# Inputs with the heads of a position side by side in DRAM, and the input and gated tiles of a float32r feed-forward shifted by 192 bytes against its weights

## The chip, the cores and the metric

One Trainium2 chip, one of its cores. The metric is the device time of one execution in microseconds, as the median of the runs; what the host does with the arrays before the launch is outside it.

## The reference

A linear attention with a complex decay, followed by a gated feed-forward. There are 4 batches, 8 heads, 768 positions and 48 channels per head; the feed-forward has 3072 tokens, 384 inputs and 1536 hidden columns.

```python
mag = np.sqrt(a_re * a_re + a_im * a_im)
scale = np.minimum(mag, 0.999) / (mag + 1e-06)
a_re_n, a_im_n = (a_re * scale, a_im * scale)
...
for t in range(S):
    ar, ai = (a_re_n[:, :, t, :, None], a_im_n[:, :, t, :, None])
    new_re = ar * S_re - ai * S_im
    new_im = ar * S_im + ai * S_re
    kv = np.einsum('bhd,bhe->bhde', k[:, :, t], v[:, :, t])
    S_re, S_im = (new_re + kv, new_im)
    y[:, :, t] = np.einsum('bhd,bhde->bhe', q[:, :, t], S_re)
...
x = np.ascontiguousarray(attn_out.transpose(0, 2, 1, 3)).reshape(B * S, H * D)
...
g = x @ w_gate
silu = g * (1.0 / (1.0 + np.exp(-g)))
val = x @ w_val
return (silu * val @ w_out).astype(np.float32)
```

The inputs q, k, v, a_re and a_im come as (batch, head, position, channel) float32; the three weights come as float64 and reach the chip as pairs of 32-bit words.

## The kernel before, in words

**Work.** The sequence is cut into 24 slabs of 128 positions (6 chunks of 4 batches). Two slabs form one of 12 groups, g = 0 to 11. For a group, `stage_ops` loads a_re, a_im, q and k (positions on the partitions, heads and channels in the row, `load` at L342, issued by SP), takes logarithms and arctangents on ACT, sums them along the positions with matmuls against a triangle (L445), and scales q and k by the results. `slab_ops` turns q and k (six slabs with TensorE transposes, L569; later ones with DVE's 32x32 transposes and shuffling DMAs `T<-ww`, L598), loads v (`ldv`, L606), makes the scores (L618) and their product with v (L649, into p_py), and updates the carried state (L676). The copy of p_py to SBUF is the transposed input of the feed-forward: `xh`, its rounding to float32r (L658), and `xl`, the rest (L665), 3 k-tiles of 128 channels by 256 positions.

**Feed-forward.** `ffn_ops` runs a group's feed-forward in 12 blocks f of 128 hidden columns. For g > 0 a block has 18 matmuls at L829: gate and value, 3 k-tiles, and three products each (weights' high part with xh, high part with xl, low part with xh). The weight tile is the stationary operand (128 columns, 512 bytes of a partition), xh or xl the moving one (256 columns). ACT takes the silu (L835), DVE multiplies (L840), and `hh` and `hl` are again a float32r rounding and its rest (L299 or L301, L295). Then 6 matmuls at L863 add the block to the two output banks; here hh or hl is stationary (128 of its 256 columns) and the row of w_out moves (384 columns). Group 0 does the same with whole float32 numbers and a third of the matmuls.

**Weights.** `weight_ops` loads the 64-bit words of block f into a tile (L719) and joins them to float32 on DVE (c1 to c3, L728 to L736). `split_ops` later writes their high and low float32r parts (c4, c5) into the place of the block before: `place("w", f - 1)`. So block f reads the tile ww(f-1) and wo(f-1).

**Addresses.** `place` lets the weights of place f begin `STARTS[f]` floats (0 to 56, so 0 to 224 bytes) behind the start of their tile, and the tiles of xh, xl, hh and hl have no such offset. All these tiles come from one pool, one behind the other in each partition. From the start addresses that the program gives them, the weights of L829 lie behind xh and xl, modulo 512 bytes, by 0, 400, 416, 176, 320, 336, 352, 384, 416, 448, 96 and 392 bytes for the blocks f = 0 to 11. The stationary hh and hl of L863 lie behind the moving row of w_out by 0, 112, 224, 208, 192, 176, 160, 128, 352, 64, 416 and 120 bytes. All steps within a tile (k-tiles, high and low part, gate and value, the second half of hh) are multiples of 512 bytes, so the distance is the same for all matmuls of a block.

**Order.** `Planner.plan` puts all operations in one order from written-out costs and due times, which neither addresses nor the layout in DRAM enter; each engine takes its instructions in that order. SP issues every DMA: inputs, weights, and the small transfers through DRAM of a chunk's last row (`dr` and `dec`, L466 and L472; `fr`, L523; `cy`, L490). After group 1 the weights are also read once more for a check of their range (`range_ops`, L777 to L786), and a_re and a_im of the first chunk for another check (`sector_ops`, L800). `general` is a slow way for other data; it isn't taken here.

**Rows of DRAM.** In `x[b0:b0 + many, :, c * P:c * P + P, :]` a position's channels of one head are 48 floats, 192 bytes, and the next head's lie 768 positions further. A load of two slabs (384 KB) is 2048 pieces of 192 bytes.

Of the kernel before, what the change touches and what calls it, by code (L numbers as in the profile page):

```python
# [42 lines left out]

STARTS = {-1: 0, 0: 4, 1: 8, 2: 12, 3: 16, 4: 20, 5: 24, 6: 32, 7: 40, 8: 48, 9: 56, 10: 2, 11: 0}
HIGH, LOW, WHOLE = 0, 1, 2
# [131 lines left out]


def flat(t):
    return t.rearrange("p h d -> p (h d)")  # L180
# [10 lines left out]
def quick(ctx, tc, q, k, v, a_re, a_im, w_gate, w_val, w_out, out, count):  # L191
# [27 lines left out]
    def place(nm, f, dtype):  # L219

        at = STARTS[f]
        t = work.tile([P, 2 * WIDE[nm] + -(-at // 64) * 64], dtype, name=f"w{nm}{f}", tag=f"w{nm}{f}", bufs=1)
        return t[:, at:at + 2 * WIDE[nm]]

# [7 lines left out]
    def weight(nm, f, part):  # L232
# [5 lines left out]
        if nm == "o":  # L238
# [6 lines left out]
             "hh": ([P, 2 * P], F32R), "hl": ([P, 2 * P], F32R), "ost": ([P, DM], F32),  # L245
             "sc": ([P, 4, P], F32), "T": ([96, 2, H * P], F32), "dec": ([96, 4 * H], F32),
             "qs": ([P, 2 * H, 96], F32), "ks": ([P, 2 * H, 96], F32)}
# [27 lines left out]
    def new(tag, inst):  # L275
        if tag in fixed:
            t = fixed[tag][0]
        elif tag[0] in ("ww", "wo"):
            t = None
        elif tag in PSUMS:  # L280
            t = psum.tile([P, 512], F32, name="p_" + tag, tag=tag, bufs=2 if tag == "po" else slots[tag])
        else:
            shape, dt = SHAPE[tag]
            if isinstance(inst, tuple) and inst[0] in SPLIT:
                dt = F32R
            if tag == "xh" and inst == 0:
                dt = F32
            if tag == "xl" and isinstance(inst, str):
                dt = U32
            t = work.tile(shape, dt, name=tag, tag=tag, bufs=slots[tag])  # L290
        at_[tag, inst] = t
        return t
# [26 lines left out]
    def stage_ops(g, first, many):  # L319
# [19 lines left out]
        def load(t, x):  # L339
            def fn(e):  # L340
                b0 = 2 * bp + first
                nc.sync.dma_start(out=new(*tg(t)), in_=x[b0:b0 + many, :, c * P:c * P + P, :].rearrange("b h t d -> t (b h) d"))  # L342
            pl.add(f"ld_{t}{N}", {"SP": 0.55}, fn, deps=[held.get(t, "")], alloc=[tg(t)], lat=1.4, move=1.09 * many)
# [198 lines left out]
    def slab_ops(n):  # L542
# [61 lines left out]
        def ldv(e):  # L604
            at_["vt", n] = vts[n % 2]
            nc.sync.dma_start(out=vts[n % 2][:, :, 0:D], in_=v[b, :, c * P:c * P + P, :].rearrange("h t d -> t h d"))  # L606
        pl.add("ldv" + N, {"SP": 0.55}, ldv, deps=[f"ldv{n - 1}"] if n else [], alloc=[("vt", n)], lat=1.4, move=1.09)
# [182 lines left out]
    def sector_ops(g):  # L790
# [7 lines left out]
        for t, x, tags in (("re", a_re, both), ("im", a_im, parts)):  # L798
            def ld(e, x=x, t=t):
                nc.sync.dma_start(out=at(t).rearrange("p (h d) -> p h d", d=D), in_=x[b0:b0 + 2, :, 0:P, :].rearrange("b h t d -> t (b h) d"))  # L800
            pl.add(f"kl{t}" + N, {"SP": 0.55}, ld, alloc=tags, lat=1.4, move=2.18, deps=[f"c5{NF - 1}o", f"f2_0.{NF - 1}", f"c5{NF - 1}w", f"f1_0.{NF - 1}"])
# [149 lines left out]
def general(ctx, tc, q, k, v, a_re, a_im, w_gate, w_val, w_out, out):  # L951
# [7 lines left out]
    with ExitStack() as first:  # L959
# [13 lines left out]
        with tc.For_i(0, S, TB) as t0:  # L973
            part = {}
            for nm, src in (("q", q), ("k", k), ("re", a_re), ("im", a_im)):
                part[nm] = two.tile([P, TB, DQ], F32, name="g_" + nm)
                for j in range(4):
                    nc.sync.dma_start(out=part[nm][32 * j:32 * j + 32],
                                      in_=src.rearrange("b h t d -> (b h) t d")[:, bass.ds(t0, TB), j * DQ:(j + 1) * DQ])
            vv = two.tile([P, TB, D], F32, name="g_v")  # L980
            for j in range(4):
                nc.sync.dma_start(out=vv[32 * j:32 * j + 32], in_=v.rearrange("b h t d -> (b h) t d")[:, bass.ds(t0, TB), :])
            mag, den = two.tile([P, TB, DQ], F32, name="g_mag"), two.tile([P, TB, DQ], F32, name="g_den")
# [127 lines left out]
```

## Time and profile before

| | us |
|---|---|
| median of 3 runs | 662.51 (660.56 to 663.02) |
| span of the profiled execution, first to last instruction | 657.5 |
| the median less that span | 5.0 |
| TensorE matmuls (PE) busy | 622.8 (95% of the span) |
| weight loads (PEld) busy | 582.5 (89%) |
| VectorE (DVE) busy | 499.6 (76%) |
| ScalarE (ACT) busy | 398.2 (61%) |
| DMA queue of the loads and stores, share of 16 engines | 49.2% |

The profile gives the profiled execution's span, and no time of its own around it; the 5.0 us are the difference to the median of the runs shown. Busy time counts an instruction from its start to its modelled end, so matmuls that follow each other without a gap overlap in it. The trace names operands by tile, out<-in; at L829 `p_gv<-xh,ww` is a matmul with xh moving and ww stationary. [...]

### The profile page before, as it was taken

The numbers are of one execution on the slowest core, as the hardware profiler recorded it, in microseconds if no ns is written. First come the engines' busy times: TensorE is split into PE (matmuls) and PEld (weight loads), VectorE is DVE, ScalarE is ACT, GpSimd is POOL, SyncE is SP. The second block draws the span as 40 slices with busy tenths as digits, with TensorE's granted clock in tenths as the row PEclk, the third lists the DMA queues.
The fourth block names the chain that finished last, engine by engine and source line by source line (L and its number), as shares of the span: only waits on it lengthen the run. The fifth ranks groups of instructions, "written<-read, shape, count | busy, mean of one in ns | idle before, by whom it ended". The sixth has DMA issues, their size and how long they took to land.

```text
span 657.5 us, 15503 instructions
## 1 busy us (share of the span) xinstructions
PE 622.8 (95%) x6306; PEld 582.5 (89%) x6306; DVE 499.6 (76%) x923; ACT 398.2 (61%) x654; POOL 3.0 (0%) x9
## 2 busy tenths in 40 slices
PE   2689999999999999999999999999999999999996
PEld 0367787899998999999999999999999999999995
DVE  8799999989876976976976976966876966643332
ACT  7865159876885866756956756967847836211110
POOL 1000000000000000000000000000000000000000
PEclk9999999999999999999999999999999999999998
DMA  9999602356645655655655656645543530320000
GB/s 181 293 286 287 169 25 55 53 111 117 164 105 125 165 120 128 153 138 122 159 131 122 153 130 130 141 126 122 123 105 63 126 85 16 77 52 1 25 1 29
DMA packets 234932, 77.49 MB, mean 118 GB/s; under 512 B 208859, under 2 KB 230621, under 8 KB 234854
## 3 DMA queue, kind: packets, MB, share of 16 engines
q1 hardware_dynamic: 234854, 76.43, 49.2%
q8 instruction: 51, 0.84, 0.5%
q14 instruction: 27, 0.22, 0.1%
HBM read 57.47 MB, written 4.78 MB: 95 GB/s over the span
## 4 chain that ended last, share of the span: by engine, by line
PE 66%; DVE 16%; DMA 8%; ACT 5%; issue 3%; SPq 1%; DVEq 0%; ACTq 0%
PE p_gv L829 35%; PE p_po L863 17%; PE p_py L649 5%; PE p_ps L618 5%; ACT L946 2%; DMA wo<-in_moe_w_val_dram 2%; PE p_pm L676 2%; ACT s L350 2%; PE p_pm L445 2%; DVE xl L732 1%; DMA wo<-in_moe_w_out_dram 1%; DVE sg L840 1%; DVE s L295 1%; DVE sc L624 1%; SPq L719 1%
## 5 line engine op out<-in xcount | busy, mean ns | idle before, releaser
L829 PE MATMUL p_gv<-xh,ww 128*128 128x256 f32 x1596 | 314.7, 293 | 1.3 <-DVE sg L840 1.1
L829 PEld LDWEIGHTS p_gv<-xh,ww 128*128 128x128 f32 x1596 | 258.1, 189 | 9.8 <-DVE sg L840 3.2
L829 PE MATMUL p_gv<-xl,ww 128*128 128x256 f32 x726 | 203.6, 280 | 0.0
L946 ACT ACT_TABLE_LOAD x111 | 142.4, 1283 | 1.9
L829 PEld LDWEIGHTS p_gv<-xl,ww 128*128 128x128 f32 x726 | 136.6, 188 | 0.1
L835 ACT ACTIVATE sg<-p_gv 128x256 f32<-128x256 f32 x144 | 54.0, 382 | 136.3 <-PE p_gv L829 135.3
L863 PE MATMUL p_po<-wo,hh 128*128 128x384 f32 x484 | 127.0, 343 | 0.0
L840 DVE TENSOR_TENSOR sg<-sg,p_gv 128x256 f32<-128x256 f32 x144 | 58.7, 414 | 62.4 <-ACT sg L835 62.4
L863 PEld LDWEIGHTS p_po<-wo,hh 128*128 128x128 f32 x484 | 81.5, 188 | 2.3 <-issue 2.2
L863 PE MATMUL p_po<-wo,hl 128*128 128x384 f32 x242 | 81.6, 337 | 0.0
L295 DVE TENSOR_TENSOR hl<-sg,hh 128x256 fp32r<-128x256 f32 x132 | 54.4, 418 | 6.8 <-ACT hh L299 1.5
L618 PE MATMUL p_ps<-T 96*128 96x128 f32 x384 | 53.2, 279 | 0.0
L618 PEld LDWEIGHTS p_ps<-T 96*128 96x128 f32 x384 | 50.6, 196 | 0.9 <-ACT T L299 0.3
L863 PEld LDWEIGHTS p_po<-wo,hl 128*128 128x128 f32 x242 | 45.5, 188 | 0.0
L299 ACT CAST hh<-sg 128x256 fp32r<-128x256 f32 x49 | 19.7, 403 | 34.7 <-DVE sg L840 27.9
L350 ACT ACTIVATE s<-s 128x768 f32<-128x768 f32 x44 | 36.7, 842 | 5.2 <-DVE s L295 4.7
L781 DVE TENSOR_REDUCE flags<-wo 128x1 f32<-128x384 f32 x36 | 19.8, 549 | 25.2 <-DMA wo<-in_moe_w_val_dram 11.3
L649 PE MATMUL p_py<-sc,vt 128*32 128x128 f32 x768 | 37.1, 273 | 1.5 <-ACT xh L658 0.9
L624 DVE TENSOR_TENSOR sc<-p_ps,tri 128x512 f32<-128x512 f32 x48 | 32.7, 682 | 4.0 <-PE p_ps L618 3.6
L649 PE MATMUL p_py<-T,G 96*32 96x128 f32 x640 | 33.5, 281 | 0.0
L786 ACT ACTIVATE wo<-wo 128x384 f32<-128x384 f32 x36 | 20.2, 562 | 12.6 <-DMA wo<-in_moe_w_out_dram 5.7
L829 PE MATMUL p_gv<-xh,ww-1_412 128*128 128x256 f32 x132 | 26.1, 287 | 1.7 <-ACT xh L658 1.7
(134 smaller groups left out, 800.9 us busy)
## 6 DMA issues: line engine op xcount, KB each, us to landing
T<-ww SPq DMA_DIRECT2D x216, 64.0 KB, 2.1
wo<-in_moe_w_out_dram SPq DMA_DIRECT2D x24, 384.0 KB, 5.9
ww<-in_moe_w_gate_dram SPq DMA_DIRECT2D x12, 384.0 KB, 5.9
vt<-in_v_dram SPq DMA_DIRECT2D x24, 192.0 KB, 4.3
ww<-in_moe_w_val_dram SPq DMA_DIRECT2D x12, 384.0 KB, 6.7
out_dram<-ost SPq DMA_DIRECT2D x24, 192.0 KB, 2.3
wo<-in_moe_w_gate_dram SPq DMA_DIRECT2D x12, 384.0 KB, 3.6
wo<-in_moe_w_val_dram SPq DMA_DIRECT2D x12, 384.0 KB, 4.0
```

The costliest lines, as they stand in the source:

```text
L295: V[e].tensor_tensor(out=out, in0=a, in1=b, op=op)
L350: nc.scalar.activation(out=of(dst), in_=of(source), func=func, scale=scale, **kw)
L618: nc.tensor.matmul(out=ps[:, hh, :], lhsT=kT(4 * qd + hh), rhs=qT(4 * qd + hh), start=True, stop=True)
L624: nc.vector.tensor_tensor(out=s, in0=at_["ps", f"{n}.{qd}"].rearrange("p (h t) -> p h t", h=4), in1=mask.unsqueeze(1).to_broadcast([P, 4, ...
L649: nc.tensor.matmul(out=o, lhsT=l, rhs=r, start=opens, stop=closes, tile_position=(0, 32 * slot))
L781: nc.vector.tensor_reduce(out=flags[:, fl_lo + j:fl_lo + j + 1], in_=high(1), axis=AX.X, op=ALU.min, apply_absolute_value=True)
L786: nc.scalar.activation(out=high(0), in_=high(1), func=AF.Square, accum_out=flags[:, fl_hi + j:fl_hi + j + 1])
L829: nc.tensor.matmul(out=gv[:, i, :], lhsT=l, rhs=r, start=(m == 0), stop=(m == len(mm) - 1))
L835: nc.scalar.activation(out=new("sg", I), in_=at_["gv", I][:, 0:2 * P], func=AF.Silu)
L840: nc.vector.tensor_tensor(out=sg, in0=sg, in1=at_["gv", I][:, 2 * P:4 * P], op=ALU.mult)
L863: nc.tensor.matmul(out=po, lhsT=l[:, cs], rhs=weight("o", f, part), start=f == 0 and j == 0, stop=f == NF - 1 and j == len(products) - 1)
L946: nc.scalar.preload_act_table_set(op.load)
```

## The change

Three things. First, the host hands over the five attention inputs as (batch, position, head, channel). All heads of a position are then one run of 384 floats (1536 bytes), and the loads take it as one piece; the tile's rows are the same as before. Only v's tile keeps a pitch of 64 floats per head, so its destination still has pieces of 48 floats. Second, the weight tiles begin at the start of their places (no `STARTS`), and the tiles of xh, xl, hh and hl get 128 floats more, of which the data begin 48 floats (192 bytes) in. Third, the small `dec` tile is padded to 512 bytes. The order of the plan stays: none of its inputs is touched.

By the sizes in the code, every tile of that pool is then a multiple of 512 bytes (ww 6144, wo 3072, xh and xl 3584, hh and hl 1536, dec 512, and the rest 1024, 1536, 2048, 3072, 6144 or 8192). So the weights of L829 lie 320 bytes (512 - 192) behind xh and xl in all 12 blocks, and hh and hl lie 192 bytes behind w_out in all. Between two blocks, where the next stationary operand is hh under a moving xh, or ww under a moving w_out, the distance is 0. The tiles sc, T, ks and qs move by 128 bytes, modulo 512, against vt and G, which stay.

```diff
-STARTS = {-1: 0, 0: 4, 1: 8, 2: 12, 3: 16, 4: 20, 5: 24, 6: 32, 7: 40, 8: 48, 9: 56, 10: 2, 11: 0}
+SHIFT = 48
...
+def rows(x, b0, many, c):
+    return x[b0:b0 + many, c * P:c * P + P].rearrange("b t h d -> t b (h d)")
...
     def place(nm, f, dtype):
 
-        at = STARTS[f]
-        t = work.tile([P, 2 * WIDE[nm] + -(-at // 64) * 64], dtype, name=f"w{nm}{f}", tag=f"w{nm}{f}", bufs=1)
-        return t[:, at:at + 2 * WIDE[nm]]
+        return work.tile([P, 2 * WIDE[nm]], dtype, name=f"w{nm}{f}", tag=f"w{nm}{f}", bufs=1)
...
-             "sc": ([P, 4, P], F32), "T": ([96, 2, H * P], F32), "dec": ([96, 4 * H], F32),
+             "sc": ([P, 4, P], F32), "T": ([96, 2, H * P], F32), "dec": ([96, P], F32),
...
-            t = work.tile(shape, dt, name=tag, tag=tag, bufs=slots[tag])
+            if tag in ("xh", "xl", "hh", "hl"):
+                n = math.prod(shape[1:])
+                t = work.tile([P, n + P], dt, name=tag, tag=tag, bufs=slots[tag])[:, SHIFT:SHIFT + n]
+                if len(shape) > 2:
+                    t = t.rearrange("p (k n) -> p k n", k=shape[1])
+            else:
+                t = work.tile(shape, dt, name=tag, tag=tag, bufs=slots[tag])
+                if tag == "dec":
+                    t = t[:, 0:4 * H]
...
-                nc.sync.dma_start(out=new(*tg(t)), in_=x[b0:b0 + many, :, c * P:c * P + P, :].rearrange("b h t d -> t (b h) d"))
+                nc.sync.dma_start(out=new(*tg(t)).rearrange("p (b h) d -> p b (h d)", b=many), in_=rows(x, b0, many, c))
...
-            nc.sync.dma_start(out=vts[n % 2][:, :, 0:D], in_=v[b, :, c * P:c * P + P, :].rearrange("h t d -> t h d"))
+            nc.sync.dma_start(out=vts[n % 2][:, :, 0:D], in_=v[b, c * P:c * P + P])
...
-                nc.sync.dma_start(out=at(t).rearrange("p (h d) -> p h d", d=D), in_=x[b0:b0 + 2, :, 0:P, :].rearrange("b h t d -> t (b h) d"))
+                nc.sync.dma_start(out=at(t).rearrange("p (b n) -> p b n", b=2), in_=rows(x, b0, 2, 0))
...
-        a = _np.ascontiguousarray(inputs[name])
+        a = _np.asarray(inputs[name])
+        a = _np.ascontiguousarray(a.transpose(0, 2, 1, 3) if a.ndim == 4 else a)
```

The loads of `general` are rewritten to the same order of the axes.

## Rows read from the trace of the kernel before

**Rows 1.** The page, busy time of each engine and the chain by line
```profile
PE 622.8 (95%) x6306; PEld 582.5 (89%) x6306; DVE 499.6 (76%) x923; ACT 398.2 (61%) x654; POOL 3.0 (0%) x9
...
PE p_gv L829 35%; PE p_po L863 17%; PE p_py L649 5%; PE p_ps L618 5%; ACT L946 2%; DMA wo<-in_moe_w_val_dram 2%; PE p_pm L676 2%; ACT s L350 2%; PE p_pm L445 2%; DVE xl L732 1%; DMA wo<-in_moe_w_out_dram 1%; DVE sg L840 1%; DVE s L295 1%; DVE sc L624 1%; SPq L719 1%
```

**Rows 2.** Stretches: window, length, each engine's busy us (instructions), granted clock, DMA share, GB/s
```profile
60.00:80.00 20.00, 20.00 (x164) 15.69 (x163) 20.00 (x38) 6.73 (x12) 0.00 (x0) 1.00 0.77 218
...
350.00:400.00 50.00, 50.00 (x556) 48.60 (x556) 40.52 (x75) 34.91 (x58) 0.00 (x0) 1.00 0.56 130
```

**Rows 3.** PE at L829, one window per block of group 11 (blocks 2, 4, 9)
```profile
617.16:619.47 2.31, 2.31 (x18) 2.11 (x18) 1.00 0.34 127
...
623.54:625.75 2.21, 2.21 (x18) 2.02 (x18) 1.00 0.00 0
...
639.40:641.60 2.20, 2.20 (x18) 2.01 (x18) 1.00 0.00 0
...
sum 27.34, PE 27.31 PEld 24.97; mean PE 2.28 PEld 2.08
```

**Rows 4.** L829, last 14 matmuls of block 4 in each of 11 groups
```profile
174.43:176.16 1.73, 1.73 (x16) 1.55 (x14) 1.00 1.15 235
228.24:230.03 1.79, 1.79 (x16) 1.60 (x14) 1.00 0.66 138
...
sum 19.18, PE 19.18 PEld 17.18; mean PE 1.74 PEld 1.56
```

**Rows 5.** L829, last 14 matmuls of block 9 in each of 11 groups
```profile
149.16:150.96 1.80, 1.80 (x16) 1.61 (x14) 1.00 0.00 0
...
402.42:404.16 1.74, 1.74 (x16) 1.56 (x14) 1.00 1.06 217
```

**Rows 6.** PE at L863, windows of blocks 0 to 9 of group 11 (blocks 4, 7)
```profile
631.96:633.15 1.19, 1.19 (x6) 0.88 (x6) 1.00 0.00 0
...
641.44:642.66 1.22, 1.22 (x6) 0.90 (x6) 1.00 0.00 0
...
sum 12.06, PE 12.05 PEld 8.91; mean PE 1.21 PEld 0.89
```

**Rows 7.** The page, GB/s in 40 slices; DMA issues with KB and us to landing
```profile
GB/s 181 293 286 287 169 25 55 53 111 117 164 105 125 165 120 128 153 138 122 159 131 122 153 130 130 141 126 122 123 105 63 126 85 16 77 52 1 25 1 29
...
T<-ww SPq DMA_DIRECT2D x216, 64.0 KB, 2.1
...
out_dram<-ost SPq DMA_DIRECT2D x24, 192.0 KB, 2.3
...
im<-in_a_im_dram SPq DMA_DIRECT2D x11, 384.0 KB, 5.0
...
s<-fr SPq DMA_DIRECT2D x9, 384.0 KB, 3.7
```

**Rows 8.** Chain of waits, 0 to 60 us: start us, us, what
```profile
0.82 3.16 DMA ww<-in_a_re_dram
...
21.39 3.04 DMA fr<-ww
```

**Rows 9.** Timeline of DVE, 0 to 62 us: start us, us, what, [idle before]
```profile
19.78 0.56 DVE L295 TENSOR_TENSOR ww<-ww,wo 128x384 f32<-128x384 f32 x1
...
25.01 0.56 DVE L295 TENSOR_TENSOR ks<-wo,ww 128x384 f32<-128x384 f32 x1 [2.39 <-ACT ww L350]
```

**Rows 10.** Timeline of SP's issues, 0 to 75 us
```profile
16.75 0.78 SPq L466 DMA_DIRECT2D dr<-ww  x1
...
20.42 0.86 SPq L472 DMA_DIRECT2D dec<-dr  x2
```

**Rows 11.** Chain of waits, 200 to 232 us
```profile
201.51 6.10 DMA im<-in_a_im_dram
```

**Rows 12.** Timeline of PE, 210 to 216 us
```profile
213.77 0.39 PE L829 MATMUL p_gv<-xh,ww-1_412 128*128 128x256 f32 x1 [1.66 <-ACT xh L658]
214.96 0.39 PE L829 MATMUL p_gv<-xl,ww-1_412 128*128 128x256 f32 x1 [0.80 <-DVE xl L665]
```

More of the change, by code (lines that the diff above doesn't have):

```diff
@@ L977, in general @@
                 for j in range(4):
-                    nc.sync.dma_start(out=part[nm][32 * j:32 * j + 32],
-                                      in_=src.rearrange("b h t d -> (b h) t d")[:, bass.ds(t0, TB), j * DQ:(j + 1) * DQ])
+                    for b in range(B):
+                        nc.sync.dma_start(out=part[nm][32 * j + H * b:32 * j + H * b + H],
+                                          in_=src[b, bass.ds(t0, TB), :, j * DQ:(j + 1) * DQ].rearrange("t h d -> h t d"))
             vv = two.tile([P, TB, D], F32, name="g_v")
             for j in range(4):
-                nc.sync.dma_start(out=vv[32 * j:32 * j + 32], in_=v.rearrange("b h t d -> (b h) t d")[:, bass.ds(t0, TB), :])
+                for b in range(B):
+                    nc.sync.dma_start(out=vv[32 * j + H * b:32 * j + H * b + H],
+                                      in_=v[b, bass.ds(t0, TB)].rearrange("t h d -> h t d"))
             mag, den = two.tile([P, TB, DQ], F32, name="g_mag"), two.tile([P, TB, DQ], F32, name="g_den")
```

## The prediction

> **What bounds the kernel now.** I read the busy times and the chain first. PE is busy for 95% of the span, and the chain that ended last is mostly TensorE: 35% of the span is L829 and 17% L863 [rows 1]. [...]
>
> The rows that decide the case are the blocks of the last group, where nothing but L829 and L863 runs [rows 3]. All twelve L829 windows hold the same 18 matmuls and 18 weight loads, at clock 1.00, and yet block 2 takes 2.31 us and blocks 4 and 9 take 2.21 and 2.20. What differs from block to block is where the weights begin. Block 4 is the one at a distance of 320 bytes, which the change gives to all. Over the 11 groups its last 14 matmuls take 1.73 to 1.74 us nine times and 1.79 us twice (at 228 us for one) [rows 4], and nothing lies in between. So there is a short and a long rhythm: 0.06 us over 13 intervals, 4.6 ns each, 0.08 us over a block of 17 intervals. Block 9, at 448 bytes, is in the short one three times of 11 (from 402 us on) and else at 1.79 to 1.80 [rows 5]. No other block is ever in it. The distance thus makes the short rhythm likely, not certain.
>
> [...]
>
> **The change, part by part.**
>
> *L829, 132 blocks (groups 1 to 11).* The twelve windows sum to 27.31 us [rows 3]. In that group blocks 4 and 9 were both short; with block 9 short in 3 of 11 and block 4 in 9 of 11 a mean group has 27.38. After the change all blocks are like block 4: 12 x 2.205, and 2 in 11 of them 0.08 longer, 26.63 us. That is 0.75 us a group and 8.2 us over 11 groups. Bounds: all short, 27.38 - 26.46 = 0.92, 10.1 us in all; all long, 12 x 2.285 = 27.4, nothing. I take the share that block 4 shows, as the same distance is the nearest row there is.
>
> *L863, 132 blocks.* Ten undisturbed windows sum to 12.05, 1.205 each; block 4, at a distance of 192 as all will be, has 1.19 and the slowest 1.22 [rows 6]. 0.015 x 132 gives 2.0 us; the lower bound is nothing.
>
> *The seams between the blocks.* There the distance becomes 0. Block 2's 2.31 against the long rhythm's 2.285 is 1.5 ns a matmul, 1.22 against 1.205 is 3 ns; with one of each kind per block, about 5 ns x 132 = 0.7 us lost.
>
> *Other matmuls.* sc and T move by 128 bytes against vt and G, at L649 (5% of the span on the chain, 33 us [rows 1]). No row shows it at another distance. With half of L829's spread, 2.5% either way, it is 0.8 us up or down; I take 0, as nothing tells the sign. Group 0's float32 blocks get other distances too; 2.5% of the 40 us from 60 to 100 us would be 1.0 either way, but DVE is full beside them [rows 2] and would have to be faster as well; 0. The scores at L618 read both operands from T, whose parts keep their distance; 0.
>
> *The first loads.* The first 16 us are DMA-bound: with 192-byte pieces the queue moves 181 GB/s in the first slice, with the weights' longer ones 286 to 293 in the next three [rows 7]. The first load (a_re, 192 KB) lands 3.16 us after its issue [rows 8]; a store of 192 KB in whole rows needs 2.3 [rows 7]. So up to 0.86 us there, of which I take 0.7. The next wait is larger. DVE loses 2.39 us at 25 us to ACT [rows 9], which waits for `fr`, 3.04 us for 1.5 KB [rows 8], queued behind the inputs' and weights' backlog. `fr` also starts late: its data are ready at 20.3 us (DVE's 19.78 + 0.56 [rows 9]), but SP stands before `dec`, until `dr`, issued at 16.75, has landed at 20.4 [rows 10]. The twelve first loads are 3.07 MB, 17 us at 181 GB/s and 10.6 at 290; with 6 us less in the queue a small transfer should come near the 2.1 us of the shuffles [rows 7]. That gives 1.0 us for `fr` and 0.9 for the SP order, 1.9 of the 2.39. Together 2.6 us, carried on, because DVE and PE follow without a gap. Bounds: nothing if the weights simply move up into the queue; 0.86 + 2.39 = 3.3.
>
> *Later loads.* Most are hidden under PE. One isn't: a_im at 201.5 us lands after 6.10 us [rows 11], holds the small transfers and ACT behind it, and PE then idles 1.66 and 0.80 us [rows 12]. A 384 KB transfer with pieces of 3 KB lands in 3.7 us where a_im's median is 5.0 [rows 7]. 1.3 to 2.4 us earlier; I take 1.5 off the 2.46 of idle time (bounds 0 and 2.5). v keeps its 192-byte pieces, so nothing comes from it.
>
> *What is late next.* PE runs two per cent ahead of a plan whose order was made for the old times. DVE's 40.5 of 50 becomes 41.4 [rows 2]; waits like the two on `xh` and `xl` [rows 12] should come up in other groups. I put in 1.0 us, with bounds of 0 and twice the two, 5.
>
> Sum: -8.2 - 2.0 + 0.7 - 2.6 - 1.5 + 1.0 = -12.6 us on a span of 657.5, so 644.9; with the 5.0 us that the median of the runs has over that span, **649.9 us**.
>
> **The rivals.**
>
> *The distance is worth nothing, or every block falls into the long rhythm.* For it: two groups of 11 at 320 bytes are long, and the seams, now at distance 0, are a new way into each block. Against: nine of 11, and DMA doesn't choose (short at a share of 1.15, long at 0.66 [rows 4]). Then only the loads are left: 662.5 - 4.1 + 0.7, 659.1 us. Chance 0.10.
>
> *The short rhythm comes, but waits on DVE and ACT take it back.* For it: DVE is busy for 81% of a PE-bound stretch. Against: PE has 50.00 of 50 there. With the upper bound of the waits (5 instead of 1), 654 us. Chance 0.15.
>
> *All blocks short, and loads at their upper bounds.* -10.1 - 2.0 + 0.7 - 3.3 - 2.5 = -17.2, 645.3 us; 0.8 less if L649 also gains. Chance 0.20.
>
> *Slower.* What counts is where the moving operand itself begins, not the distance: xh and xl now start 192 bytes off, which no block of before shows. Its place is every interval of L829 and L863; its price all blocks as the slowest: (12 x 2.31 - 27.38) x 11 = 3.7 and 0.015 x 132 = 2.0, 668.2 us before any gain of the loads. It comes out slower once the loads bring under 2.4 us. Against it: the moving w_out begins at twelve different places now, and L863 hardly cares (1.19 to 1.22). Chance 0.05.
>
> *The change doesn't do what it says* where a tile breaks the multiple of 512; all sizes in the code are multiples, so I give it no chance of its own.
>
> **How the numbers follow.** The forecast has 0.50, and with the next two 0.85 lies on the faster side. A measurement of this kernel can tell about 0.5% (3.3 us) from no change: under 659.2 is faster, over 665.8 slower. The first rival sits on that edge, and I split it: faster 0.86, same 0.09, slower 0.05. The range reaches from the third rival's 645.3 with L649's 0.8 off, 644, to the case of half the rhythm and the waits' upper part, 657; it leaves out the first and the last rival, 0.15.
>
> **What would show it.** L829's windows in the last group should be 2.20 to 2.21 in nearly all blocks and their sum near 26.6; L863's near 1.19. `ww<-in_a_re_dram` should land well under 3.16 us, the wait of 2.39 us near 25 us should shrink below 1, and PE's idle time near 212 us below 1.5. First matmuls of group 1 should start about 2.6 us earlier. Wrong would be windows of 2.28 and more at an even distance, or windows that shrink while PE's idle time grows by as much.

## The result, and the profile after

The kernel after takes **653.84 us** (median of 4 runs, 652.44 to 654.78) against 661.53 of the kernel before on the same chip (660.27 to 663.02); the ratio is 0.9887 [0.9860, 0.9913]. It is faster by 1.1%, inside the forecast range, and 3.9 us above the forecast of 649.9. The span went from 657.5 to 651.3, so 6.2 us, where the working had 12.6. The profiled run of after took 652.97 us, 1.7 us more than its span, where the forecast had put 5.0 around it.

All lines behind the new functions moved: L829 is L839 now, L863 is L873, L618 is L628.

The page of after (busy times, and the chain by line, which answer to [rows 1]):

```profile
PE 619.1 (95%) x6306; PEld 578.3 (89%) x6306; DVE 498.9 (77%) x923; ACT 397.5 (61%) x654; POOL 2.9 (0%) x9
...
PE p_gv L839 33%; PE p_po L873 16%; PE p_py L659 5%; PE p_ps L628 5%; ACT L956 2%; ACT s L360 2%; DVE xl L742 2%; DMA wo<-in_moe_w_val_dram 2%; PE p_pm L686 2%; PE p_pm L455 2%; DMA wo<-in_moe_w_out_dram 1%; DMA re<-in_a_re_dram 1%; DVE sg L850 1%; DVE sc L634 1%; DVE s L305 1%
```

TensorE is the bound as before: at 350 to 400 us it is busy for 50.00 of 50 us at a granted clock of 1.00, with DVE at 40.71 and ACT at 34.72 (before: [rows 2]). The granted clock over the span is 0.999, and was 0.997. The busy time of TensorE fell by 3.7 us only, where L829 alone should have lost 8.2.

**Where the 6.2 us are.** Busy times overlap, so I added up the time from each matmul's start to the next one's start, by line, from the first float32r matmul of the feed-forward to the last (a wait before a matmul goes to the line of the matmul ahead of it). All in us, from the two traces:

| | before | after | moved | forecast |
|---|---|---|---|---|
| start of the first such matmul (group 1) | 105.66 | 103.26 | -2.40 | -2.6 |
| L829, now L839 | 288.46 | 284.90 | -3.56 | -8.2 |
| L863, now L873 | 147.45 | 148.21 | +0.75 | -2.0 + 0.7 |
| L676, now L686, which held the stall near 212 us | 14.71 | 13.35 | -1.35 | -1.5 |
| all other lines | 94.85 | 94.97 | +0.1 | 0 |

The row for waits (+1.0 in the forecast) is missing here, since idle time stands in the lines. That matters for L863: without the idle time behind it the line went from 145.81 to 145.12, and the idle time in it from 1.65 to 3.08.

The loads came near the forecast; the feed-forward did not. The windows of the last group show it. The columns are window and length in us, busy us of PE and of its weight loads (instructions), granted clock, DMA share and GB/s, as in [rows 3]; blocks 0, 4 and 9 of L839 in group 11 of the kernel after:

```profile
604.47:606.74 2.27, 2.27 (x18) 2.08 (x18) 1.00 0.00 0
...
617.14:619.41 2.27, 2.27 (x18) 2.08 (x18) 1.00 0.00 0
...
632.97:635.24 2.27, 2.27 (x18) 2.08 (x18) 1.00 0.00 0
...
sum 27.24, PE 27.22 PEld 24.91; mean PE 2.27 PEld 2.08
```

All twelve take 2.27, and the sum went from 27.31 [rows 3] to 27.22, not to 26.6. The spread from 2.20 to 2.31 is gone, and so are the two blocks that were short. Now the same view as [rows 4], the last 14 matmuls of block 4 in each of the 11 groups, groups 1, 2, 9, 10 and 11 of after:

```profile
117.61:119.34 1.73, 1.73 (x16) 1.55 (x14) 1.00 0.20 1
171.57:173.36 1.79, 1.79 (x16) 1.61 (x14) 1.00 0.92 267
...
526.41:528.14 1.73, 1.73 (x16) 1.55 (x14) 1.00 0.18 38
572.72:574.46 1.74, 1.74 (x16) 1.55 (x14) 1.00 0.00 0
617.61:619.40 1.79, 1.79 (x16) 1.61 (x14) 1.00 0.00 0
...
sum 19.42, PE 19.42 PEld 17.40; mean PE 1.77 PEld 1.58
```

The two rhythms are still there, with nothing between them: in each of the 132 blocks the last 14 matmuls follow each other by 113.3 ns (below, a short block) or by 117.8 ns (a long one), but for one short block at 114.5. But this block, whose own distance the change left at 320 bytes, is short in 5 groups instead of 9, and over all blocks 46 of 132 are short, where I had taken 9 of 11, which is 108. What tells the groups apart is the work ahead of the block. In groups 9 and 10 it stands behind the scores (L628), in group 11 straight behind L873. Over the whole trace, 75 blocks stand straight behind L873. Of the 64 that start without a delay one is short. The other 11 have a matmul at their start that comes some 0.05 us late or more, mostly by a wait, and ten of them are short (8 of 11 in a second trace of this kernel). Behind other work it depends on the work: blocks behind L628 are short 19 times of 19, those behind L686 2 of 14.

L873 in the same group (blocks 0 and 1, and the sum of blocks 0 to 9; answers to [rows 6]):

```profile
612.92:614.13 1.21, 1.21 (x6) 0.89 (x6) 1.00 0.43 156
616.09:617.30 1.21, 1.21 (x6) 0.89 (x6) 1.00 0.00 0
...
sum 12.07, PE 12.05 PEld 8.90; mean PE 1.21 PEld 0.89
```

All even, and on the mean of before: 12.05 and 12.05 [rows 6].

**The start.** The timeline of DVE (start us, us, what, idle before; answers to [rows 9]). The first line is the first load's wait in the kernel before, the others are from the kernel after:

```profile
4.00 2.55 DVE L362 RECIPROCAL ww<-ww 128x384 f32<-128x384 f32 x1 [1.27 <-DMA ww<-in_a_re_dram]
...
3.26 2.55 DVE L372 RECIPROCAL ww<-ww 128x384 f32<-128x384 f32 x1 [0.54 <-DMA ww<-in_a_re_dram]
...
7.05 0.96 DVE L305 TENSOR_TENSOR s<-re 128x768 f32<-128x768 f32 x1 [0.36 <-DMA re<-in_a_re_dram]
...
22.17 0.55 DVE L305 TENSOR_TENSOR ks<-wo,ww 128x384 f32<-128x384 f32 x1
...
27.97 0.56 DVE L514 TENSOR_SCALAR s<-p_pm 128x384 f32<-128x384 f32 x1 [0.84 <-PE p_pm L452]
```

The wait for the first load is 0.54 instead of 1.27 (so 0.73 less, 0.7 was forecast). The 2.39 before the subtraction that makes ks [rows 9] are gone, and two new waits of 0.36 and 0.84 take 1.2 of them back. That is 1.9 us of the 2.40 by which group 1 starts earlier. The issues of SP, in the same columns, at the start and near 200 us (answers to [rows 10]; the first line is again from the kernel before):

```profile
12.34 2.02 SPq L342 DMA_DIRECT2D kt<-in_k_dram  x1
...
7.53 0.40 SPq L352 DMA_DIRECT2D kt<-in_k_dram  x1
...
14.03 0.79 SPq L476 DMA_DIRECT2D dr<-ww  x1
...
16.37 0.94 SPq L482 DMA_DIRECT2D dec<-dr  x2
17.89 0.24 SPq L533 DMA_DIRECT2D fr<-ww  x1
...
198.06 0.42 SPq L352 DMA_DIRECT2D im<-in_a_im_dram  x1
198.57 0.55 SPq L476 DMA_DIRECT2D dr<-qs  x1
```

The last of the twelve input loads is issued at 7.53 us; before, it was issued at 12.34 and took 2.02. `dec` goes 4.05 us earlier than at 20.42 [rows 10], and `fr` is no longer in the chain of waits.

**The stall near 212 us.** The timeline of PE (answers to [rows 12]):

```profile
209.13 0.38 PE L839 MATMUL p_gv<-xh,ww-1_412 128*128 128x256 f32 x1 [0.31 <-ACT xh L668]
210.31 0.39 PE L839 MATMUL p_gv<-xl,ww-1_412 128*128 128x256 f32 x1 [0.80 <-DVE xl L675]
```

The first wait fell from 1.66 to 0.31, the second stayed. The prediction had a_im holding the small transfers and ACT behind it. That is so in both traces: SP's next issue, which waits for `dr`, and ACT's first use of a_im stand side by side. Two lines of SP and one of ACT in the kernel before, then two in the kernel after:

```profile
201.51 2.73 SPq L342 DMA_DIRECT2D im<-in_a_im_dram  x1
207.82 0.90 SPq L472 DMA_DIRECT2D dec<-dr  x2
207.70 0.84 ACT L370 ACTIVATE s<-im 128x768 f32<-128x768 f32 x1 [2.12 <-DMA im<-in_a_im_dram]
...
203.57 0.90 SPq L482 DMA_DIRECT2D dec<-dr  x2
203.45 0.85 ACT L380 ACTIVATE s<-im 128x768 f32<-128x768 f32 x1 [1.37 <-DMA im<-in_a_im_dram]
```

From a_im's issue to ACT it was 6.19 us before (201.51 to 207.70) and is 5.39 now (198.06 to 203.45). The path is the one of the prediction, and the step is 0.80 us where 1.3 to 2.4 were forecast. The issue itself became short as well: it held SP for 2.73 us, now for 0.42, so `dr` follows a_im's issue by 0.51 us instead of 2.82. That alone brought `dr` nothing here, since it still comes in just behind a_im.

The view of the DMA of after, GB/s in 40 slices and one group of issues with KB and us to landing (answers to [rows 7]):

```profile
GB/s 233 314 279 361 40 26 74 60 88 124 173 99 148 151 123 115 180 118 118 188 111 118 163 131 123 146 127 119 129 105 60 127 90 16 76 51 1 25 1 29
...
im<-in_a_im_dram SPq DMA_DIRECT2D x11, 384.0 KB, 5.9
```

The 5.9 here, and the 5.0 of [rows 7], say nothing of the load near 200 us: of the eleven loads of a_im the trace tells the landing of one, the first (issued at 3.18 us, at 5.63 before). The packets fell from 234932 to 141748, and the queue's share from 49.2% to 43.6%.

### The profile page after: what moved, and what is told of

Read it like the earlier page. It is cut to its first block, busy times and chain, and to the rows that moved or that the text cites. A ratio compares the mean times of both kernels' runs of the same rounds, so it can differ in the third digit from the quotient of the medians.

```text
span 651.3 us, 15505 instructions
## 1 busy us (share of the span) xinstructions
PE 619.1 (95%) x6306; PEld 578.3 (89%) x6306; DVE 498.9 (77%) x923; ACT 397.5 (61%) x654; POOL 2.9 (0%) x9
## 2 busy tenths in 40 slices
DMA packets 141748, 77.49 MB, mean 119 GB/s; under 512 B 102363, under 2 KB 137437, under 8 KB 141670
## 3 DMA queue, kind: packets, MB, share of 16 engines
q1 hardware_dynamic: 141670, 76.43, 43.6%
## 4 chain that ended last, share of the span: by engine, by line
PE 64%; DVE 17%; ACT 7%; DMA 6%; issue 4%; SPq 1%; DVEq 0%; ACTq 0%
PE p_gv L839 33%; PE p_po L873 16%; PE p_py L659 5%; PE p_ps L628 5%; ACT L956 2%; ACT s L360 2%; DVE xl L742 2%; DMA wo<-in_moe_w_val_dram 2%; PE p_pm L686 2%; PE p_pm L455 2%; DMA wo<-in_moe_w_out_dram 1%; DMA re<-in_a_re_dram 1%; DVE sg L850 1%; DVE sc L634 1%; DVE s L305 1%
## 5 line engine op out<-in xcount | busy, mean ns | idle before, releaser
L839 PE MATMUL p_gv<-xh,ww 128*128 128x256 f32 x1596 | 311.3, 292 | 1.9 <-DVE sg L850 1.9
L839 PEld LDWEIGHTS p_gv<-xh,ww 128*128 128x128 f32 x1596 | 257.9, 190 | 10.7 <-DVE sg L850 4.1
L839 PE MATMUL p_gv<-xl,ww 128*128 128x256 f32 x726 | 202.9, 279 | 0.0
L839 PEld LDWEIGHTS p_gv<-xl,ww 128*128 128x128 f32 x726 | 136.4, 188 | 0.2 <-issue 0.2
L873 PE MATMUL p_po<-wo,hh 128*128 128x384 f32 x484 | 126.4, 342 | 0.0
L850 DVE TENSOR_TENSOR sg<-sg,p_gv 128x256 f32<-128x256 f32 x144 | 58.5, 413 | 61.0 <-ACT sg L845 60.9
L873 PEld LDWEIGHTS p_po<-wo,hh 128*128 128x128 f32 x484 | 81.2, 188 | 2.3 <-issue 2.0
L873 PE MATMUL p_po<-wo,hl 128*128 128x384 f32 x242 | 81.5, 337 | 0.0
L628 PE MATMUL p_ps<-T 96*128 96x128 f32 x384 | 53.2, 279 | 0.2 <-PE p_gv L839 0.2
L628 PEld LDWEIGHTS p_ps<-T 96*128 96x128 f32 x384 | 50.6, 196 | 1.3 <-PE p_gv L839 0.4
L873 PEld LDWEIGHTS p_po<-wo,hl 128*128 128x128 f32 x242 | 45.4, 188 | 0.0
L311 DVE CAST hh<-sg 128x256 fp32r<-128x256 f32 x83 | 23.6, 288 | 4.2 <-PE p_po L873 0.4
```

Source lines behind the costliest of these rows:

```text
L311: nc.vector.tensor_copy(out=out, in_=in_)
L628: nc.tensor.matmul(out=ps[:, hh, :], lhsT=kT(4 * qd + hh), rhs=qT(4 * qd + hh), start=True, stop=True)
L839: nc.tensor.matmul(out=gv[:, i, :], lhsT=l, rhs=r, start=(m == 0), stop=(m == len(mm) - 1))
L850: nc.vector.tensor_tensor(out=sg, in0=sg, in1=at_["gv", I][:, 2 * P:4 * P], op=ALU.mult)
L873: nc.tensor.matmul(out=po, lhsT=l[:, cs], rhs=weight("o", f, part), start=f == 0 and j == 0, stop=f == NF - 1 and j == len(products) - 1)
```

## Theory and rivals before the runs

Theory: an L829 block is short or long as a whole; at distance 320 both are possible, and the seam decides which. The seam into a block is the distance, modulo 512, at which its first stationary tile lies behind the operand that moves last ahead of it: the w_out row ahead of an L829 block, xh ahead of an L863 block. The change puts that seam at 0 in every block, and 0 leads into the long rhythm. It is the argument of the prediction's first rival. Rivals: at 320 bytes every block behind L863 is long whatever the seam; or the shorter blocks are eaten by waits.

## The experiments

### One half of the change at a time

The kernel after with the addresses of before (`STARTS` kept, no `SHIFT`), and the kernel after with the loads of before.

```diff
-SHIFT = 48
+STARTS = {-1: 0, 0: 4, 1: 8, 2: 12, 3: 16, 4: 20, 5: 24, 6: 32, 7: 40, 8: 48, 9: 56, 10: 2, 11: 0}
```

> Only the order of the inputs in DRAM and the loads are changed; the addresses in SBUF are those of the kernel before. Theory (the gain is a sum of parts: the start, the stall near 212 us, the L829 rhythm): the first matmul of group 1 comes 2.4 us earlier than before, as it did with the whole change (105.7 to 103.3), the 2.46 us of PE idle time near 212 us shrink to about 1.1, and the twelve L829 windows of the last group stay at a sum near 27.3 us; the time falls by 3 to 4 us against before (ratio 0.994 to 0.996). Rival (the loads were hidden anyway, and the addresses bring it all): group 1 starts within 0.5 us of before, ratio 0.998 to 1.002.

Measured: 655.94 us (8 runs), ratio 0.9918 [0.9889, 0.9948], so 5.4 us where 3 to 4 were expected; the interval reaches down to 3.4. Span 652.1. By the sums from start to start the first matmul of group 1 comes 2.77 us earlier than before and L676 takes 1.73 less: PE has no wait near 212 us at all, where 1.1 us were expected, and from a_im's issue to ACT it is 4.65 us. The L829 line loses 1.20, of which 0.80 is the second of those two waits [rows 12]; its windows in the last group sum to what they did before:

```profile
sum 27.34, PE 27.32 PEld 24.97; mean PE 2.28 PEld 2.08
```

```diff
-                nc.sync.dma_start(out=new(*tg(t)).rearrange("p (b h) d -> p b (h d)", b=many), in_=rows(x, b0, many, c))
+                nc.sync.dma_start(out=new(*tg(t)), in_=x[b0:b0 + many, :, c * P:c * P + P, :].rearrange("b h t d -> t (b h) d"))
```

> Only the addresses in SBUF are changed; inputs and loads are those of the kernel before. Theory (sum of parts): group 1 starts as before at 105.7 us, the PE idle time near 212 us stays near 2.5, L829 blocks come in two lengths, 13 intervals of 113.3 or of 117.8 ns, about four in ten short, and the L829 intervals sum to 3 to 4 us less than before (288.5); ratio 0.993 to 0.997. Rival (the rhythm needs the calmer DMA queue too): fewer than two in ten short, ratio 0.998 or more.

Measured: 656.86 us (12 runs), ratio 0.9942 [0.9917, 0.9966]. L829's line is 3.77 us below before, L863's 1.89 above (its waits included), the first matmul of group 1 1.03 later. The two waits near 212 us are 0.97 and 0.80, not the 2.5 expected, though the loads are those of before (6.02 us from a_im's issue to ACT); so not all of the change there need be the loads'. 45 of 132 blocks are short, behind L869 without a delay 2 of 64, behind the scores 19 of 19; the last group's windows sum to

```profile
sum 27.24, PE 27.22 PEld 24.91; mean PE 2.27 PEld 2.08
```

the same as in after. So the rhythm comes from the addresses, and no part of the DMA traffic in it shows: 45 blocks short with the loads of before, 46 and 42 with those of after. Which half is worth more stays open, as the two intervals overlap. The two ratios multiply to 0.986; the whole change has 0.9887 [0.9860, 0.9913].

### The seam varied, the distance of L829 fixed

The w_out tiles in a pool of their own, each 32 bytes longer, so that the seam into L844 (L829 of the kernel before) differs from block to block while L844's distance is 320 in all. The w_out row moves in L878 (L863 of before), so L878's own distance differs along with the seam; the seam into L878 is 0 in all.

```diff
+    pool_w = ctx.enter_context(tc.tile_pool(name="pool_w", bufs=1))
+    pool_o = ctx.enter_context(tc.tile_pool(name="pool_o", bufs=1))
+    pool_o.tile([P, 8], F32, name="gap", tag="gap", bufs=1)
+    POOL = {"w": (pool_w, 0), "o": (pool_o, 8)}
...
-        return work.tile([P, 2 * WIDE[nm]], dtype, name=f"w{nm}{f}", tag=f"w{nm}{f}", bufs=1)
+        pool, more = POOL[nm]
+        return pool.tile([P, 2 * WIDE[nm] + more], dtype, name=f"w{nm}{f}", tag=f"w{nm}{f}", bufs=1)[:, 0:2 * WIDE[nm]]
```

> As after the change, with the weights' tiles in pools of their own and each w_out tile 32 bytes longer, so that the distance of the next L829 weights behind the last moving w_out (the seam; 0 everywhere after the change) takes 12 values in steps of 32 bytes, while all L829 blocks stay at 320 bytes. Theory (the rhythm of a block is chosen by how it is entered, and behind an L863 block by the seam's distance): of the blocks that follow an L863 block without a wait, those at a seam of 0 are long (117.8 ns), those near 160 to 192 and near 64 bytes are short (113.3), as block 4 of before was behind seams of 176 and 64. Rival (a block straight behind L863 is long whatever the distance, and the short ones come only behind other work or a wait): all of them are long at every seam, as 61 of 61 were after the change.

Measured (one run): 654.19 us. Blocks straight behind L878 and without a delay, short and long, by the seam into them:

| seam | 128 | 384 | 160 | 96 | 352 | 448 | 192, 224, 256, 288, 320, 480 |
|---|---|---|---|---|---|---|---|
| short | 5 | 5 | 3 | 2 | 2 | 1 | 0 |
| long | 0 | 1 | 2 | 5 | 4 | 8 | 26 |

The rival that blocks behind L863 are long whatever the seam falls: the same block at the same distance is short at some seams. They are not those that the theory named, though: 192 has no short block, and 128 and 384 have the most.

### The distance varied, the seams aside

L844's weights at twelve distances instead of 320, the moving tiles 384 bytes in, the seam into L878 320 for all. The seam into L844 differs along with the distance, so each distance is seen at one seam behind L878; some blocks of each stand behind other work.

```diff
-SHIFT = 48
+SHIFT = {"xh": 96, "xl": 96, "hh": 48, "hl": 48}
...
+    pool_o.tile([P, 24], F32, name="gap", tag="gap", bufs=1)
+    POOL = {"w": (pool_w, 8), "o": (pool_o, 0)}
```

> As after the change, but each L829 weight tile is 32 bytes longer than the last, so that the 12 blocks stand at 12 distances from 128 to 512 bytes behind the moving xh and xl. Theory (two rhythms, open to few distances): only distances near 320 and 448 show 113.3 ns in some blocks; the others are at 117 to 120 ns in all groups. Rival (320 is not special; some distance never seen before, such as 192 to 288 or 128 to 160, gives the short rhythm in all groups, or one below 113 ns): such a distance shows up here, and a kernel with it in all blocks would be faster than both.

Measured (one run): 653.0 us, as the kernel after. Only at 320 and 448 was a block ever short (2 of 11 each, else 117.8 ns); 0, 256, 416 and 160 had 119 to 120 ns, 128 and 288 118 to 119, 224 and 480 mostly 116.7. Some of the others have more than one value too (352: 117.2 or 118.8), but none comes near 113. L844 as a whole took what it did before (-0.07 us), L878 1.68 us less than before: with the seam into it at 320 the six intervals of an undisturbed block (no interval above 0.18 us) sum to 1043 ns, against 1053 in before and 1047 in after, where that seam is 0. So the distance does what the prediction read from blocks 4 and 9, and at two distances of twelve the short rhythm was seen. It goes by the distance, not by where the moving tile begins: at 320, the same two values come with xh at the start of its tile (before), 192 bytes in (after) and 384 bytes in (here).

### The best two seams for all blocks

As after, with the gap between the pools and the start of hh chosen so that the seam into L844 is 128, and in a second kernel 384; distances 320 and 192 as in after.

```diff
-SHIFT = 48
+SHIFT = {"xh": 48, "xl": 48, "hh": 16, "hl": 16}
...
+    pool_o.tile([P, 96], F32, name="gap", tag="gap", bufs=1)
+    POOL = {"w": (pool_w, 0), "o": (pool_o, 0)}
```

(The second: `hh` and `hl` at 80, the gap 32 floats.)

> As the changed kernel, but the weight tiles stand in address space so that the step from the last weights of L878 to the first of L844 is 128 bytes modulo 512 instead of 0 (L844's own distance stays at 320, L878's own at 192, the step from L844 into L878 is 384). Theory (the seam decides the rhythm of an L844 block that stands straight behind an L878 block): the some 60 blocks that stand so and are long at seam 0 become short, 16 matmuls by about 4.5 ns each and one window less, 0.07 to 0.08 us a block: L844 as a whole 4 to 5 us less than in the changed kernel, the time 648 to 650 us, 0.980 to 0.983 of the kernel before. Rival (TensorE is no longer the bound there, the shorter blocks wait for VectorE and ScalarE): blocks short all the same, but TensorE's idle time grows by as much and the time stands within 1.5 us of the changed kernel.

> The mirror of the run beside it: the step from L878's last weights to L844's first is 384 bytes modulo 512, the step from L844 into L878 128, the distances within the lines 320 and 192 as in the changed kernel. Theory: blocks behind L878 are short here too (5 of 6 were at 384 in the run where seams vary), L844 3 to 5 us less than in the changed kernel, the time 648.5 to 651 us, 0.981 to 0.985 of the kernel before. Rival (waits give it back): within 1.5 us of the changed kernel.

> The changed kernel itself, as the measure of the two runs beside it on the same chip. Both theories: 653 to 655 us, 0.987 to 0.991 of the kernel before; of the blocks straight behind L873 nearly none short.

Measured: 651.45 us (ratio 0.9860 [0.9830, 0.9889]) and 651.59 (0.9864 [0.9833, 0.9894]) against 653.45 of the changed kernel beside them (0.9884 [0.9853, 0.9914]). Better by 2 us, where the theory had 4 to 5 and the rival under 1.5. The first two had 76 and 78 short blocks, the changed kernel 42. Behind L878 only half were short, and the windows of the last group (seam 128, blocks 0 to 3) show which half:

```profile
603.23:605.50 2.27, 2.27 (x18) 2.07 (x18) 1.00 0.00 0
606.39:608.60 2.21, 2.21 (x18) 2.02 (x18) 1.00 0.03 7
609.49:611.76 2.27, 2.27 (x18) 2.08 (x18) 1.00 0.32 115
612.65:614.86 2.21, 2.21 (x18) 2.02 (x18) 1.00 0.00 0
...
sum 26.88, PE 26.88 PEld 24.57; mean PE 2.24 PEld 2.05
```

They alternate, through the whole group, at one distance and one seam. So my theory was too simple, and the rival did not hold either. A block swaps the rhythm of the block before it: with undisturbed L878 blocks between, 24 of 26 that followed a long one were short, and 28 of 28 that followed a short one were long. So the rhythm of the block before counts, across the six matmuls of L878 (1.04 us) between the two, and I took it that the seam into L878 counts as well. In the run with varied seams, 128 had come together with 0 into L878, and there three blocks had stayed short behind a short one.

### Which pair of seams keeps the short rhythm

One kernel that varies both seams together in twelve steps of 96 bytes, distances fixed, and one that takes 0 into L878 and 128 into L844 from the earlier run. With the distances fixed at 320 and 192 the two seams always sum to 0 modulo 512. So a pair is one free number, and the first kernel can't tell which of its two steps counts.

```diff
+WO = (32, 256, 352, 448, 128, 224, 320, 416, 0, 96, 480, 64)
...
+def shift(tag, inst):
+    return 48 if tag[0] == "x" else (80 + WO[int(inst.split(".")[1])] // 4) % P
...
+    POOL = {"w": (pool_w, 0), "o": (pool_o, 24)}
```

> Distances within the lines as in the changed kernel (L850 320, L884 192), but the places of the twelve w_out tiles, and with them the start of each gated tile, go up in steps of 96 bytes, so that the step from L850 into L884 takes twelve values (32 to 480 modulo 512) and the step from L884 into L850 is its negative. Theory (a block's rhythm is set by the rhythm of the block before it together with the two steps it is entered through): every step value gives blocks behind L884 that are either all long, all short, or swap with the block before; the step 128 into L850 (384 into L884) swaps as in the run where it held for all blocks, and few values, if any, give short behind short as well as short behind long. Rival (the step into L850 alone decides by chance of the moment, the swap seen at 128 and 384 was a coincidence of the order of work): shares of 30 to 70% short at most values, whatever the block before was. The time stands near 653 us under both.

Measured (one run): 655.49 us, where about 653 was expected. Three kinds of pairs, as the theory has it. By the steps (into L884, into L850), short blocks of those that followed a long one, and of those that followed a short one:

| steps | behind long | behind short | |
|---|---|---|---|
| (192, 320) | 4 of 4 | 4 of 4 | short |
| (384, 128) | 3 of 5 | 0 of 1 | swaps |
| (96, 416) | 4 of 5 | 0 of 3 | swaps |
| (128, 384) | 1 of 1 | 0 of 3 | swaps |
| (224, 288) | 0 of 2 | 0 of 4 | long |
| (480, 32) | 0 of 3 | 0 of 2 | long |
| (64, 448) | 0 of 4 | 0 of 1 | long |

The other five had blocks of one kind alone ahead of them: (32, 480) 2 of 2 and (448, 64) 1 of 1 behind short ones, (160, 352) 0 of 7 behind short ones, (352, 160) 2 of 2 and (256, 256) 0 of 2 behind long ones. But for three single blocks, what a pair does with a given kind is the same each time, so the rival of mixed shares falls. Few values, as expected, keep a short block short.

```diff
-SHIFT = 48
+SHIFT = {"xh": 48, "xl": 48, "hh": 48, "hl": 48}
...
+    pool_o.tile([P, 96], F32, name="gap", tag="gap", bufs=1)
+    POOL = {"w": (pool_w, 0), "o": (pool_o, 0)}
```

> Steps as for the three blocks that stayed short behind a short one in the run where seams vary: 0 into L878, 128 into L844; that puts L878's own distance at 320 instead of 192, L844's stays at 320. Theory (the two steps and the block before decide together): L844 blocks behind L878 are short whatever the block before was, some 60 instead of 30 of them, 30 by 0.08 us = 2.4 us less in L844 than with the steps 384 and 128; L878's blocks take 1052 instead of 1044 ns (as that run shows for 320 and 192), 132 by 8 ns = 1.1 us more; the time some 1.3 us less than with 384 and 128, about 650 us, 0.981 to 0.985 of the kernel before. Rival (the step 128 into L844 swaps long and short whatever the step into L878 is): half of the blocks stay long and the time is 652 to 653 us, the 1.1 us of L878 added to the time with 384 and 128.

Measured: 650.84 us, ratio 0.9867 [0.9841, 0.9892]. 104 blocks short; with undisturbed L878 blocks between, 47 of 47 behind a short block stayed short, and 6 of 7 behind a long one became so. The last group's L844 sums to

```profile
sum 26.52, PE 26.51 PEld 24.25; mean PE 2.21 PEld 2.02
```

By the traces the L844 line is 2.21 us below the kernel with 384 and 128 (2.4 expected), L878's 1.04 above it (1.1 expected), the last matmul 1.19 us earlier (1.3 expected). The rival, that a seam of 128 swaps in any case, falls. The ratio, with 0.981 to 0.985 expected, is above that and wouldn't tell the kernels apart: it is as good as that of the two above.

### The pair from the scan

```diff
-SHIFT = 48
+SHIFT = {"xh": 48, "xl": 48, "hh": 96, "hl": 96}
...
+    pool_o.tile([P, 48], F32, name="gap", tag="gap", bufs=1)
+    POOL = {"w": (pool_w, 0), "o": (pool_o, 0)}
```

> From the scan of steps: step 192 into L878 and 320 into L844, the one pair there (beside the controls) that gave short blocks in number both behind a long block (4 of 4) and behind a short one (4 of 4); the distances are those of the changed kernel, 320 within L844 and 192 within L878. Theory (the two steps and the block before decide together): L844 as in the run with steps 0 and 128, 281.5 us, 3.3 us below the changed kernel and 2.2 below the pair 384 and 128, while L878 stays at the 1042 ns a block that distance 192 gives there instead of 1050, 1 us less than with steps 0 and 128; the time 649 to 650.5 us, 0.980 to 0.985 of the kernel before. Rival (eight blocks of a scan with other neighbours tell nothing of a kernel where every block is entered so): half of the blocks or fewer are short, the time 651 to 653.5 us.

Measured: **649.93 us**, ratio 0.9843 [0.9814, 0.9872], the lowest of the study, though its interval overlaps those of the three kernels above and of after. By the traces it isn't ahead of the kernel with seams 0 and 128: the last matmul starts at 641.87 us here and at 641.83 there. 115 of 132 blocks are short; counted as before, 49 of 49 behind a short one and 3 of 3 behind a long one. Windows of L844 in the last group, blocks 0 and 1 and the sum:

```profile
602.45:604.66 2.21, 2.21 (x18) 2.02 (x18) 1.00 0.00 0
605.55:607.76 2.21, 2.21 (x18) 2.02 (x18) 1.00 0.04 7
...
sum 26.58, PE 26.56 PEld 24.27; mean PE 2.21 PEld 2.02
```

26.56 is near the 26.63 that the prediction had for a group. The L844 line is at 281.49 us, 6.97 below before. TensorE gives some of it back: L878 stands 2.16 above before, though its undisturbed blocks take 1042 ns and not 1053. The idle time that stands in this line rose from 1.65 to 4.33 us. Without idle time the line is 0.99 us below that of the kernel with seams 0 and 128, as expected, but its idle time is 1.28 longer. The stretch 450 to 500 us of this kernel, as in [rows 2]:

```profile
450.00:500.00 50.00, 49.34 (x602) 47.12 (x601) 39.00 (x74) 33.47 (x52) 0.00 (x0) 1.00 0.40 96
```

PE's 49.34 of 50 us say that it is no longer full. Its waits from 100 us on (who waits for whom: us in total, times, longest):

```profile
PE p_gv L844 <- DVE sg L855: 2.6, 5, 0.7
PE p_po L878 <- DVE sg L855: 1.3, 1, 1.3
PE p_pm L460 <- DVE s L521: 1.3, 1, 1.3
```

and the same view of the kernel after, then two lines of the kernel before:

```profile
PE p_gv L839 <- DVE sg L850: 1.9, 5, 0.5
PE p_po L873 <- DVE sg L850: 1.3, 1, 1.3
PE p_gv L579 <- DVE T L311: 1.3, 2, 0.8
PE p_pm L455 <- DVE s L516: 0.9, 2, 0.7
...
PE p_gv L829 <- DVE sg L840: 1.1, 3, 0.4
PE p_pm L445 <- DVE s L506: 0.4, 2, 0.2
```

The wait of L844 for the gated product and that of L460 for DVE's s sum to 3.9 us here, to 2.8 in after (L839, L455) and to 1.5 in before (1.1 and 0.4). So what the second rival described is there, and small: where the blocks are shorter, some of the gain comes back as such waits.

All versions by the trace, with the time between starts of the two lines (L829 and L863 of the kernel before):

| kernel | short blocks of 132 | L829 us | L863 us | median us | ratio |
|---|---|---|---|---|---|
| before | 12 | 288.46 | 147.45 | 661.53 | 1 |
| loads alone | 13 | 287.26 | 147.54 | 655.94 | 0.9918 |
| addresses alone | 45 | 284.69 | 149.34 | 656.86 | 0.9942 |
| after (two traces) | 46, 42 | 284.90, 285.48 | 148.21, 148.42 | 653.84, 653.45 | 0.9887, 0.9884 |
| seams 384 and 128 | 76 | 283.77 | 148.27 | 651.45 | 0.9860 |
| seams 128 and 384 | 78 | 283.74 | 147.81 | 651.59 | 0.9864 |
| seams 0 and 128, L863 at 320 | 104 | 281.56 | 149.32 | 650.84 | 0.9867 |
| seams 192 and 320 | 115 | 281.49 | 149.61 | 649.93 | 0.9843 |

The medians come from several chips; the ratio is against the kernel before on the same one.

## Why the prediction was right in its sign and range, and what failed in it

**L829, -8.2: the step that failed.** It is the sentence "I take the share that block 4 shows, as the same distance is the nearest row there is". The two rhythms, their size (113.3 and 117.8 ns, 4.5 where the text had 4.6) and the distance of 320 as what allows the short one were right; the distance varied in twelve steps shows the last. But the share of 9 in 11 was that of one block with its own seams, and the change moved the seams of all blocks to 0. There a block that follows L863 without a delay stays long (63 of 64 in the kernel after). The short blocks went from 12 to 46, not to 108, and the line lost 3.56 us. The last kernel shows it: with other seams and the same distances 115 blocks are short, and a group sums to 26.56.

**The seams, +0.7.** They were priced as one slow interval of 5 ns per block. The first rival named them as "a new way into each block" and gave that 0.10. It is this rival's mechanism that acted, half of it: not every block fell into the long rhythm, since the 68 that stand behind other work or start with a delay are entered otherwise (45 of them are short), and the long rhythm at 320 (117.8) is itself below the mean of before (long blocks stood at up to 120.4). Hence a time between the rival's 659.1 and the forecast.

**L863, -2.0.** Undisturbed blocks went from 1053 to 1047 ns, 0.8 us over 132. Here too the seam was the rest: 1041 with seams 384 and 128.

**The loads, -2.6 and -1.5.** -2.40 and -1.35, and -2.77 and -1.73 in the kernel with the loads alone. Of the first, 1.9 us are the waits that the prediction named (0.73 and 2.39 less, 1.20 back). In the second the path was right and its step too large: 0.80 us from a_im's issue to ACT instead of 1.3 to 2.4; what made up the rest is not shown. "A_im's median" of 5.0, from which that step was worked out, is one load at the start. But a_im does come sooner: 4.65 to 5.99 us from issue to ACT in the ten traces with the new loads, 6.19 and 6.02 in the two with those of before. At the start the first slice moves 233 GB/s instead of 181 [rows 7].

**Waits, +1.0.** The gaps between matmuls after 100 us sum to 6.95 us before and 7.29 after; without the two near 212 us that is 4.49 and 6.18, +1.7.

**Around the span, +5.0.** No run shows such a time. Every run that has both its time and its span on record, those of the kernel before among them, takes 1.7 to 1.8 us more than its span. The other 3.3 of the 5.0 say that the profiled execution of before was shorter than the median of its runs. With 1.7 the working gives 646.6, and the profiled run of after took 652.97: 6.4 us too much gain within the span. The 3.3 too much around it hid half of the miss, so that the forecast came within 3.9 us of the median is partly luck.

**The two rhythms, by addresses alone.** The same 18 matmuls at clock 1.00 take 2.21 us with the seams at (192, 320) and 2.27 at (0, 0). What in the chip makes the two rhythms no run here shows.

## What to carry to other kernels

Where matmuls of the same kind follow each other at two spacings, look at the spacing block by block and then at what stood ahead of the block: the relative addresses of stationary and moving operand, within the block and at its seams, were worth some 0.8% here (ratio 0.9918 with the loads alone, 0.9843 with the best seams), of which the change (0.9887) reached about two fifths. A share read from one block holds for that block's entry as well as for its distance (block 4, at 320 bytes in both kernels, is short in 9 of 11 groups before and in 5 of 11 after), so an edit that makes all distances alike should be costed with the seams it makes alike. And a load in short pieces can hold its issuing queue, too (2.73 us for a_im near 200 us, 0.42 in long pieces): look at the issue's own time as well as at the landing, and at the one load in question, since a median may rest on a single landing (that of a_im, on one load of eleven).

## What the runs showed of the hardware that was not expected

- Two rhythms and next to nothing between at a distance of 320: 113.3 and 117.8 ns for 128x256 float32r matmuls, kept to the end of a block of 18.
- Of the blocks straight behind L863 that start some 0.05 us late or more, ten of 11 are short in the kernel after (8 of 11 in a second trace), and one of the 64 that start without a delay.
- The rhythm of a block goes with that of the block before it, across six matmuls of a different line, 1.04 us long: swapped 52 of 54 times at seams (384, 128), kept short 49 of 49 times at (192, 320) and 47 of 47 at (0, 128) with L863 at 320.
- The issue of one load on SP took 2.73 us with 2048 pieces of 192 bytes and 0.42 with 256 of 1536 bytes (a_im, near 200 us). Not each is held: the eleven such issues took 0.37 to 2.73 us before and 0.37 to 0.49 after.
